# A dilated FIR with gate and projection: from a window planner with two-way splits to a fixed block order with taps i and i+8 in four products

## The chip, the core and the metric

The kernel runs on one core of one Trainium2 chip. Times are device microseconds of that core. One execution is also taken by the hardware profiler; views of its profile and trace are quoted below.

## What is computed

`x` is [2, 16000, 144], `w` is [15, 144, 288], `w_o` is [144, 144], all bf16. A causal convolution with 15 taps, 2 tokens apart, is followed by a gate and a projection:

```python
dil = 2
pad = (K - 1) * dil
xp = jnp.pad(x, ((0, 0), (pad, 0), (0, 0)))
h = sum over i of einsum('btc,cd->btd', xp[:, pad - i*dil : pad - i*dil + T], w[i])
f = h[..., :D]
g = h[..., D:]
z = jnp.tanh(f) * sigmoid(g)
return z @ w_o
```

So h at token t is the sum over i of x[t - 2i] w[i]. The 144 input channels are 128 that fill TensorE's rows ("main") and 16 left over ("rest"); the rests of several taps are stacked into one 128-row operand.

## The kernel before

**Tiling.** Each sequence of 16000 tokens is cut into windows: 15 of 1024 tokens (`k4`), one of 512 (`k2`), one of 128 (`std`). Two k4 windows make a chunk; 16 chunks are run in one loop (L416). A chunk's x is loaded by two transposing DMAs (L136 to L158): `xn` with channels 0 to 127 on the partitions, `xb` with channels 16 to 143, and eight copies within SBUF (L154) stack the last 16 channels, shifted by 0, 4, ... 28 tokens, into `rx`. All of these are issued on SP's queue.

**Fewer products.** A FIR with taps in pairs can be had for two output tokens from three products rather than four: one of a sum of weights, two of differences of x. `unit_k4` (L334) does this twice, so that a window's tokens of one parity, 4 outputs of 128 tokens each, need nine accumulation groups: `a1`, `a2`, `a3`, `c1`, `b1`, `b2`, `b3`, `c2`, `c3`, each of 4 or 5 matmuls of 288 columns in a PSUM bank of its own. The stationary operand is always x or a difference of it, read with a step of 8 tokens (L339); the moving one is a weight or a sum of weights. VectorE makes the differences `en`, `fn`, `gn`, `re` of a whole chunk (L164 to L183) as dense bf16 operations and adds the groups in f32 (L350 to L382); ScalarE copies a1, c1, b1 out of PSUM (L345, L358, L366). `unit_k2` does one such step, `unit_std` none. All matmuls of the convolution are recorded at the helper's line, L319.

**Gate and projection.** ScalarE takes tanh and sigmoid of 4 x 144 outputs (L324, L325), VectorE multiplies (L326). z goes to DRAM (L275) and comes back through two transposing DMAs (L280) as `zta` and `ztb`, 72 channels each; two matmuls of 144 columns a 128-token group (L307, L308) give the output, which ScalarE copies to bf16 (L309) and stores on its own queue. The last chunk transposes z on TensorE instead (L253).

**Order.** The order of the work is left to the framework's scheduler, with two kinds of ordering added by hand: `dma_T` and `dma_plain` (L118, L128) make every transposing DMA wait for the plain ones issued since the last, and plain ones for the last transposing one. The next chunk's differences and the previous chunk's projection are spread over the units of the current chunk (L466 to L473).

Of the kernel before, what the change touches and what calls it, by code (L numbers as in the profile page):

```python
# [8 lines left out]
BF16 = mybir.dt.bfloat16  # L9
# [6 lines left out]
def kernel(  # L16
# [6 lines left out]
):  # L23
    nc = tc.nc
# [4 lines left out]
    assert D2 == 2 * D and w.shape[1] == D  # L29
    CM = 128  # L30
    CR = D - CM
    assert CR == 16 and K == 15
    DH = D // 2
    KV = 8
    KO = 7
    NG = 8
    BOFF = D - P
    HTOK = 32
    assert T % P == 0 and T >= 4 * P
    dep_sync = mybir.DependencyInfo(mybir.DependencyClass.Sync, mybir.DependencyReason.DATA)  # L40
    dep_order = mybir.DependencyInfo(mybir.DependencyClass.NoSync, mybir.DependencyReason.SCHED_ONLY)

    KIND_TOK = {"k4": 8 * P, "k2": 4 * P, "std": P}

    def mk_items():
        items = []
        t = 0
        for kind in ("k4", "k2", "std"):
            n = KIND_TOK[kind]
            while T - t >= n:  # L50
                items.append((kind, t))
                t += n
        assert t == T
        return items

    CTOK = 2 * KIND_TOK["k4"]

    def mk_chunks():
        items = mk_items()
        groups = []  # L60
        i = 0
        while i < len(items):
            j = i
            span = 0
            while j < len(items) and span + KIND_TOK[items[j][0]] <= CTOK:
                span += KIND_TOK[items[j][0]]
                j += 1
            rest = sum(KIND_TOK[it[0]] for it in items[j:])
            if rest < KIND_TOK["k4"]:
                j = len(items)  # L70
            groups.append(items[i:j])
            i = j
        res = []
        for g in groups:
            t_a = g[0][1]
            t_b = g[-1][1] + KIND_TOK[g[-1][0]]
            res.append((g, t_a, t_b))
        return res

    def chunk_geom(t_a, t_b):  # L80
        if t_a == 0:
            R = min((t_b + 15) // 16 * 16, T)
            return R, 0, HTOK
        R = (t_b - t_a + HTOK + 15) // 16 * 16
        return R, t_b - R, 0

    chunk_list = mk_chunks()
    WB = 0
    SLOT = 0
    for (_, t_a, t_b) in chunk_list:  # L90
        R, t_lo, jlo = chunk_geom(t_a, t_b)
        assert t_lo >= 0 and t_lo + R <= T
        WB = max(WB, jlo + R)
        SLOT = max(SLOT, t_b - t_a)
    WB = (WB + 15) // 16 * 16
    SLOT = (SLOT + 15) // 16 * 16
    ZPAD = 16
    all_chunks = [(b, items, t_a, t_b) for b in range(B) for (items, t_a, t_b) in chunk_list]
    NCH = len(all_chunks)
# [3 lines left out]
    xd_pool = ctx.enter_context(tc.tile_pool(name="xd", bufs=2))  # L103
    cp_pool = ctx.enter_context(tc.tile_pool(name="cp", bufs=3))
    y_pool = ctx.enter_context(tc.tile_pool(name="y", bufs=3))
    act_pool = ctx.enter_context(tc.tile_pool(name="act", bufs=2))
    z_pool = ctx.enter_context(tc.tile_pool(name="z", bufs=4))
    zt_pool = ctx.enter_context(tc.tile_pool(name="zt", bufs=2))
    os_pool = ctx.enter_context(tc.tile_pool(name="os", bufs=4))
    ztd_pool = ctx.enter_context(tc.tile_pool(name="ztd", bufs=2))  # L110
    ps_acc = ctx.enter_context(tc.tile_pool(name="ps_acc", bufs=6, space=bass.MemoryType.PSUM))
    ps_out = ctx.enter_context(tc.tile_pool(name="ps_out", bufs=2, space=bass.MemoryType.PSUM))
    dram = ctx.enter_context(tc.tile_pool(name="dram", bufs=1, space=bass.MemoryType.DRAM))

    fence_plain = []
    last_T = [None]

    def dma_T(out_ap, in_ap):  # L118
        ti = nc.sync.dma_start_transpose(out=out_ap, in_=in_ap)  # L119
        for prev in fence_plain:  # L120
            tc.add_manual_dep(ti.ins, prev, dep_sync, reason="dma batching")
        fence_plain.clear()
        if last_T[0] is not None:
            tc.add_manual_dep(ti.ins, last_T[0], dep_order, reason="dma batching")
        last_T[0] = ti.ins.name
        return ti

    def dma_plain(eng, out_ap, in_ap, track=True):  # L128
        di = eng.dma_start(out=out_ap, in_=in_ap)  # L129
        if last_T[0] is not None:  # L130
            tc.add_manual_dep(di.ins, last_T[0], dep_sync, reason="dma batching")
        if track:
            fence_plain.append(di.ins.name)
        return di

    def load_chunk(ci, cp_eng):  # L136
        b, items, t_a, t_b = all_chunks[ci]
        R, t_lo, jlo = chunk_geom(t_a, t_b)
        xn = xa_pool.tile([P, WB], BF16, name="xn")
        xb = xa_pool.tile([P, WB], BF16, name="xb")  # L140
        rx = xa_pool.tile([P, WB], BF16, name="rx")
        wv = jlo + R
        if jlo > 0:
            nc.gpsimd.memset(xn[:, 0:jlo], 0.0)
            nc.gpsimd.memset(xb[:, 0:jlo], 0.0)
# [10 lines left out]
        for l_ in lasts.values():  # L156
            fence_plain.append(l_.ins.name)
# [31 lines left out]
    def derive_chunk(cur):  # L189
        for f in derive_steps(cur):  # L190
            f()
# [325 lines left out]
```

## Time and profile before

| what | value |
|---|---|
| median of 3 runs | 389.66 us (389.6 to 389.79) |
| profiled execution, span from first to last instruction | 387.7 us |
| mean granted TensorE clock | 0.997 |
| ScalarE busy | 189.4 us (49%) |
| DMA | 60.27 MB, 143475 packets, mean 155 GB/s |
| SP's queue (x, rx, z back) | 40.87 MB, 58.7% of 16 engines' time |
| ScalarE's queue (weights, z out, stores) | 18.88 MB, 13.6% |
| convolution matmuls of 288 columns | 2598 |
| projection matmuls and z transposes on TensorE | 526 |

Of a group of instructions the profile gives the number, the mean duration of one, and the idle time of its engine just before them with what ended it. A duration runs from an instruction's start to its end; instructions of one engine can overlap, so that the distance of starts, read from the timeline, is shorter. The chain of waits goes back from the last instruction through whatever released each step: 71% of it is TensorE, 13% VectorE, 5% DMA.

### The profile page before, as it was taken

The numbers are of one execution on the slowest core, as the hardware profiler recorded it, in microseconds if no ns is written. First come the engines' busy times: TensorE is split into PE (matmuls) and PEld (weight loads), VectorE is DVE, ScalarE is ACT, GpSimd is POOL, SyncE is SP. The second block draws the span as 40 slices with busy tenths as digits, with TensorE's granted clock in tenths as the row PEclk, the third lists the DMA queues.
The fourth block names the chain that finished last, engine by engine and source line by source line (L and its number), as shares of the span: only waits on it lengthen the run. The fifth ranks groups of instructions, "written<-read, shape, count | busy, mean of one in ns | idle before, by whom it ended". The sixth has DMA issues, their size and how long they took to land.

```text
span 387.7 us, 8354 instructions
## 1 busy us (share of the span) xinstructions
PE 364.3 (94%) x3124; PEld 354.1 (91%) x3124; DVE 331.1 (85%) x753; ACT 189.4 (49%) x448; POOL 4.7 (1%) x28
## 2 busy tenths in 40 slices
PE   0669999999999999999999999999999999999995
PEld 0468998999999999999989999999999999999984
DVE  3489999998989999899859989999898989897651
ACT  4223445446454644546444454546545454654544
POOL 3000000000000000000000000000000000000000
PEclk9999999999999999999999999999999999999998
DMA  5865794596858859598798979696877969590602
GB/s 154 141 124 104 153 188 87 149 213 170 182 150 156 165 164 191 161 171 175 174 175 132 203 155 198 164 218 137 189 149 174 166 162 200 129 148 30 188 16 110
DMA packets 143475, 60.27 MB, mean 155 GB/s; under 512 B 131275, under 2 KB 133819, under 8 KB 143435
## 3 DMA queue, kind: packets, MB, share of 16 engines
q1 hardware_dynamic: 132764, 40.87, 58.7%
q10 hardware_dynamic: 10671, 18.88, 13.6%
q8 instruction: 24, 0.39, 0.4%
q14 instruction: 16, 0.13, 0.1%
HBM read 1.29 MB, written 18.03 MB: 50 GB/s over the span
## 4 chain that ended last, share of the span: by engine, by line
PE 71%; DVE 13%; DMA 5%; ACT 5%; issue 3%; ACTq 1%; SPq 1%; DVEq 0%
PE out_ps L307 4%; PE out_ps L308 3%; DMA xb<-in_x_dram 3%; ACT th L324 2%; ACTq L129 1%; DMA rx<-xb 1%; ACT sg L325 1%; PE v_ps L319 1%; DMA wo_p<-in_w_dram 1%; DVE en L166 1%; PE yo_ps L319 1%; DVE fn L176 1%; DVE re L171 1%; PE ye_ps L319 1%; SPq L119 1%
## 5 line engine op out<-in xcount | busy, mean ns | idle before, releaser
L319 PEld LDWEIGHTS <-gn 128*128 128x128 bf16 x900 | 116.0, 144 | 0.5 <-issue 0.3
L319 PEld LDWEIGHTS <-en 128*128 128x128 bf16 x540 | 67.0, 141 | 3.5 <-issue 2.6
L319 PEld LDWEIGHTS <-fn 128*128 128x128 bf16 x480 | 61.2, 144 | 2.6 <-DVE fn L176 1.8
L319 PEld LDWEIGHTS <-xn 128*128 128x128 bf16 x302 | 36.1, 136 | 13.6 <-DMA xn<-in_x_dram 11.8
L307 PE MATMUL out_ps<-wo_sb,zta 72*128 72x144 bf16 x237 | 38.7, 226 | 1.5 <-ACT os_2884 L309 0.7
L308 PE MATMUL out_ps<-wo_sb,ztb 72*128 72x144 bf16 x237 | 37.9, 227 | 0.0
L319 PEld LDWEIGHTS <-re 112*128 112x128 bf16 x248 | 35.3, 143 | 1.2 <-DVE re L171 1.1
L308 PEld LDWEIGHTS <-ztb 72*128 72x128 bf16 x237 | 31.4, 143 | 5.2 <-issue 2.3
L307 PEld LDWEIGHTS <-zta 72*128 72x128 bf16 x237 | 32.8, 144 | 0.1
L171 DVE TENSOR_TENSOR re<-rx 128x2078 bf16<-128x2078 bf16 (+1 forms) x16 | 19.3, 1206 | 5.8 <-DMA rx<-xb 5.8
L166 DVE TENSOR_TENSOR en<-xn 128x2078 bf16<-128x2078 bf16 (+1 forms) x16 | 19.3, 1205 | 1.9 <-DMA xn<-in_x_dram 1.9
L319 PEld LDWEIGHTS <-rx 128*128 128x128 bf16 (+1 forms) x128 | 18.0, 142 | 1.9 <-DMA rx<-xb 1.8
L182 DVE TENSOR_TENSOR gn<-en 128x2074 bf16<-128x2074 bf16 (+1 forms) x16 | 19.3, 1206 | 0.1
L176 DVE TENSOR_TENSOR fn<-xn 128x2076 bf16<-128x2076 bf16 (+1 forms) x16 | 19.3, 1204 | 0.0
L319 PE MATMUL a_192<-ss,xn 128*128 128x288 bf16 x4 | 1.2, 447 | 11.8 <-DMA xn<-in_x_dram 11.8
L229 DVE COPY s_main<-w_all 128x288 bf16<-128x288 bf16 x1 | 0.2, 234 | 6.6 <-DMA w_all<-in_w_dram 6.6
L260 DVE COPY zt_sb<-zt_ps 72x512 bf16<-72x512 bf16 (+1 forms) x7 | 2.6, 394 | 3.7 <-PE zt_ps L258 3.7
L146 POOL MEMSET rx<- 128x32 bf16 x16 | 1.8, 122 | 302.3 <-PE a_449 L319 33.3
L319 PE MATMUL v_ps<-s_main,xn 128*128 128x288 bf16 x32 | 4.7, 286 | 0.0
L319 PE MATMUL h_ps<-w_all,xn 128*128 128x288 bf16 x30 | 4.7, 286 | 0.0
L319 PE MATMUL yo_ps<-w_all,en 128*128 128x288 bf16 x32 | 4.6, 286 | 0.0
L319 PE MATMUL ye_ps<-wo_neg,en 128*128 128x288 bf16 x28 | 4.4, 286 | 0.0
(1922 smaller groups left out, 987.8 us busy)
## 6 DMA issues: line engine op xcount, KB each, us to landing
rx<-xb SPq DMA_DIRECT2D x14, 65.0 KB, 2.7
rx<-xb SPq DMA_DIRECT2D x14, 64.8 KB, 2.6
rx<-xb SPq DMA_DIRECT2D x14, 64.5 KB, 4.0
rx<-xb SPq DMA_DIRECT2D x14, 64.2 KB, 2.8
rx<-xb SPq DMA_DIRECT2D x13, 64.9 KB, 2.9
rx<-xb SPq DMA_DIRECT2D x13, 64.6 KB, 2.6
rx<-xb SPq DMA_DIRECT2D x13, 64.4 KB, 3.0
rx<-xb SPq DMA_DIRECT2D x13, 64.1 KB, 3.2
```

Of the source, the lines that this page charges most:

```text
L119: ti = nc.sync.dma_start_transpose(out=out_ap, in_=in_ap)
L129: di = eng.dma_start(out=out_ap, in_=in_ap)
L166: nc.vector.tensor_tensor(out=en[:, 0:wv - 2], in0=xn[:, 2:wv], in1=xn[:, 0:wv - 2], op=ALU.subtract)
L171: nc.vector.tensor_tensor(out=re[:, 0:wv - 2], in0=rx[:, 2:wv], in1=rx[:, 0:wv - 2], op=ALU.subtract)
L176: nc.vector.tensor_tensor(out=fn[:, 0:wv - 4], in0=xn[:, 4:wv], in1=xn[:, 0:wv - 4], op=ALU.subtract)
L182: nc.vector.tensor_tensor(out=gn[:, 0:wv - 6], in0=en[:, 4:wv - 2], in1=en[:, 0:wv - 6], op=ALU.subtract)
L260: nc.vector.tensor_copy(out=sb[:, 0:ne], in_=ps[:, 0:ne])
L307: nc.tensor.matmul(po[:, e, :], lhsT=ck["zta"][0:DH, sl], rhs=wo_sb[:, 0, :], start=True, stop=False)
L308: nc.tensor.matmul(po[:, e, :], lhsT=ck["ztb"][0:DH, sl], rhs=wo_sb[:, 1, :], start=False, stop=True)
L319: nc.tensor.matmul(ps[:, 0:D2], lhsT=l, rhs=r, start=(i == 0), stop=(i == n - 1))
L324: nc.scalar.activation(out=th[:, 0:ne, :], in_=y_ap[:, :, 0:D], func=ACT.Tanh)
L325: nc.scalar.activation(out=sg[:, 0:ne, :], in_=y_ap[:, :, D:D2], func=ACT.Sigmoid)
```

## The change

The two sequences are laid behind each other with a gap of 32 zero tokens and cut into 21 blocks of 1536 tokens: 32 periods of 48 tokens. Every instruction is pinned to the order in which the program gives it (`K_`).

- **Split.** Taps i and i + 8 (16 tokens apart) are taken together: four products V, A for `S` (sum), `D` (difference) and twice `E` give three outputs 16 tokens apart in a period of 48. Inside each product the taps 4 apart (8 tokens) are split again: a V group of 4 matmuls, and two A groups of 4 main matmuls (3 in one case) and one rest matmul, from `S4`, `D4`, `E4` and `Sr`, `Dr`, `Er`. An accumulator `acc` is a pair of PSUM banks; three pairs are in use, and two banks for the projection.
- **Derived operands.** `S`, `D`, `E`, `Sr`, `Dr`, `Er` are made by VectorE from xn and rx through the view `per`, which reads for each pair of tokens u the 32 periods, 48 tokens apart, 2 tokens from each, and written densely. The stationary operand of every matmul is then 128 contiguous columns.
- **Joins.** ScalarE takes eight accumulators of a block out to bf16 (two negated); VectorE joins them in bf16 SBUF operations of 1152 elements and takes the last four accumulators straight from PSUM. W2 and the other combined weights carry a factor 2, undone by `scale=0.5` in the gate.
- **z.** The block's z lies in SBUF as [128, 12 x 144], padded to 1792, and is transposed from there in one DMA on SP's queue; two matmuls with a shifted copy of w_o (`wo_ab`) make each 128-token group. z's buffer in DRAM and the fences between plain and transposing DMAs are gone.
- **Queues.** x, rx, the z transposes and the output stores are all on SP's queue, in program order; the weights and 16 pieces of w_o are loaded on ScalarE's queue ahead of the first block. The stores write runs of 288 bytes.

```diff
-        y_sb = y_pool.tile([P, 4, D2], F32, name="y4")
-        a1 = acc_tile("a1")
-        mm_group(a1, [(st(xn, -8 * j), ss[:, j, :]) for j in range(4)])
...
-        for (dst, c0) in ((zta, 0), (ztb, DH)):
-            srcz = bass.AP(zs_dram.tensor, zs_dram[slot, r0, c0].offset, [[D, ntok], [1, P]])
-            dma_T(dst[:, 0:ntok], srcz)
...
+    def load_x(bi):
+        loads, zeros = segs(bi)
+        cur = dict(bi=bi)
+        for (nm, c0) in (("xn", 0), ("xb", D - P)):
+            t_ = xa_pool.tile([P, XA], BF16, name=nm)
+            cur[nm] = t_
+            for (a, e) in zeros:
+                K_(nc.gpsimd.memset(t_[:, a:e], 0.0))
+            for (col, b, tk, n) in loads:
+                src = bass.AP(x.tensor, x[b, tk, c0].offset, [[D, n], [1, P]])
+                K_(nc.sync.dma_start_transpose(out=t_[:, col:col + n], in_=src))
+        blocks[bi] = cur
+    def load_r(bi):
+        cur = blocks[bi]
+        rx = xr_pool.tile([P, XA], BF16, name="rx")
+        for i in range(8):
+            K_(nc.sync.dma_start(out=rx[CR * i:CR * (i + 1), 16:XW], in_=cur["xb"][P - CR:P, 16 - 2 * i:XW - 2 * i]))
+        cur["rx"] = rx
+    def per(t_, s, wd):
+        return t_[:, s:s + NB_TOK].rearrange("p (k u e) -> p u k e", k=NP, e=2)[:, 0:wd // 2]
+    def uke(t_):
+        return t_[:].rearrange("p (u k e) -> p u k e", k=NP, e=2)
+    def tt(out_, a, b, op):
+        return K_(nc.vector.tensor_tensor(out=out_, in0=a, in1=b, op=op))
...
+        def s4(nm, wd):
+            s = cur[nm]
+            tt(mk(nm + "4", wd)[:], s[:, 8 * NP:(8 + wd) * NP], s[:, 0:wd * NP], ALU.subtract)
+        def sS():
+            tt(uke(mk("S", 30)), per(xn, HALO - 14, 30), per(xn, HALO + 2, 30), ALU.add)
+        def sD():
+            tt(uke(mk("D", 30)), per(xn, HALO - 14, 30), per(xn, HALO + 2, 30), ALU.subtract)
+        def sE():
+            tt(uke(mk("E", 46)), per(xn, HALO + 2, 46), per(xn, HALO - 30, 46), ALU.subtract)
+        def sS4():
+            s4("S", 22)
+        def sD4():
+            s4("D", 22)
+        def sE4():
+            s4("E", 38)
+        def sSr():
+            tt(uke(mk("Sr", 16)), per(rx, HALO, 16), per(rx, HALO + 16, 16), ALU.add)
+        def sDr():
+            tt(uke(mk("Dr", 16)), per(rx, HALO, 16), per(rx, HALO + 16, 16), ALU.subtract)
+        def sEr():
+            tt(uke(mk("Er", 32)), per(rx, HALO + 16, 32), per(rx, HALO - 16, 32), ALU.subtract)
+        return dict(S=sS, D=sD, E=sE, S4=sS4, D4=sD4, E4=sE4, Sr=sSr, Dr=sDr, Er=sEr)
...
+    load_x(0)
+    load_r(0)
+    load_x(1)
+    wo_ab = const.tile([P, 16, D], BF16)
+    K_(nc.gpsimd.memset(wo_ab[:], 0.0))
+    for j in range(8):
+        o = 16 * j
+        K_(nc.scalar.dma_start(out=wo_ab[o:P, j, :], in_=w_o[0:P - o, :]))
+        K_(nc.scalar.dma_start(out=wo_ab[0:CR + o, 8 + j, :], in_=w_o[P - o:D, :]))
+    zs = [const.tile([P, ZW], BF16, name=f"z{i}") for i in range(2)]
+    for z_ in zs:
+        K_(nc.gpsimd.memset(z_[:, NCL * D:ZW], 0.0))
+    load_r(1)
+    load_x(2)
...
+    for nm in ("S", "D", "S4", "D4"):
+        st0[nm]()
+    for (m, op) in ((0, ALU.add), (1, ALU.subtract)):
+        tt(G[m][:, 0:7, :], w_all[:, 0:7, :], w_all[:, 8:15, :], op)
+        K_(nc.scalar.copy(out=G[m][:, 7, :], in_=w_all[:, 7, :]))
+        tt(H[:, m], G[m][:, 0:4, :], G[m][:, 4:8, :], ALU.add)
+        tt(Wr[:, m, 1, :], wrA[:], wrB[:], op)
+        K_(nc.scalar.mul(out=Wr[:, m, 0, :], in_=Wr[:, m, 1, :], mul=-1.0))
+    K_(nc.scalar.mul(out=W2[:, 0:8], in_=w_all[:, 0:8], mul=2.0))
+    K_(nc.scalar.mul(out=W2[:, 8:K], in_=w_all[:, 8:K], mul=2.0))
+    for (m, src) in ((2, wrA), (3, wrB)):
+        K_(nc.scalar.mul(out=Wr[:, m, 1, :], in_=src[:], mul=2.0))
+        K_(nc.scalar.mul(out=Wr[:, m, 0, :], in_=src[:], mul=-2.0))
+    for nm in ("Sr", "Dr", "E", "E4", "Er"):
+        st0[nm]()
+    tt(H[:, 2], W2[:, 0:4, :], W2[:, 4:8, :], ALU.add)
+    tt(H[:, 3, 0:3], W2[:, 8:11, :], W2[:, 12:15, :], ALU.add)
+    K_(nc.vector.tensor_copy(out=H[:, 3, 3, :], in_=W2[:, 11, :]))
...
+    def pe_V(cur, m):
+        acc = ps_acc.tile([P, 2, 512], F32, name="acc")
+        t_ = cur[XN[m]]
+        for b1 in range(2):
+            jobs = []
+            for i in range(4):
+                o = XB[m] + SH[m] + 4 * b1 - 2 * i
+                jobs.append((t_[:, o * NP:(o + 4) * NP], H[:, m, i, :]))
+            mm_bank(acc[:, b1, 0:D2], jobs)
+        return acc
+    def pe_A(cur, m, b2):
+        acc = ps_acc.tile([P, 2, 512], F32, name="acc")
+        t_ = cur[XN[m] + "4"]
+        r_ = cur[XN[m] + "r"]
+        for b1 in range(2):
+            jobs = []
+            for i in range(4):
+                wt = Gw(m, i if b2 else i + 4)
+                if wt is None:
+                    continue
+                o = XB[m] + SH[m] + 4 * b1 - 2 * i - (0 if b2 else 8)
+                jobs.append((t_[:, o * NP:(o + 4) * NP], wt))
+            o = RB[m] + SH[m] + 4 * b1 + 8 * b2
+            jobs.append((r_[:, o * NP:(o + 4) * NP], Wr[:, m, b2, :]))
+            mm_bank(acc[:, b1, 0:D2], jobs)
+        return acc
...
+    def act_ev(dst, acc, sign=1.0):
+        K_(nc.scalar.activation(out=dst, in_=acc[:, :, 0:D2], func=ACT.Copy, scale=sign))
+    def bc(v):
+        return bass.AP(v.tensor, v.offset, [list(v.ap[0]), [0, 2]] + [list(p) for p in v.ap[1:]])
+    def gate_act(cur, f):
+        th = g_pool.tile([P, 4, D], BF16, name="th")
+        sg = g_pool.tile([P, 4, D], BF16, name="sg")
+        y = cur["y"]
+        K_(nc.scalar.activation(out=th[:], in_=y[:, 4 * f:4 * f + 4, 0:D], func=ACT.Tanh, scale=0.5))
+        K_(nc.scalar.activation(out=sg[:], in_=y[:, 4 * f:4 * f + 4, D:D2], func=ACT.Sigmoid, scale=0.5))
+        cur["g", f] = (th, sg)
+    def gate_mul(cur, f):
+        th, sg = cur["g", f]
+        z = zs[cur["bi"] % 2]
+        tt(z[:, 4 * f * D:(4 * f + 4) * D], th[:].rearrange("p a d -> p (a d)"), sg[:].rearrange("p a d -> p (a d)"),
+           ALU.mult)
+    def start_zT(cur):
+        zT = zt_pool.tile([P, ZW // P, P], BF16, name="zT")
+        K_(nc.sync.dma_start_transpose(out=zT[:], in_=zs[cur["bi"] % 2][:]))
+        cur["zT"] = zT
+        cur["os"] = os_pool.tile([P, NCL, D], BF16, name="os")
+    def outproj(cur, g):
+        po = ps_out.tile([P, 512], F32, name="po")
+        for j in range(3):
+            c = 3 * g + j
+            blk, o = divmod(D * c, P)
+            mm_bank(po[:, j * D:(j + 1) * D], [(cur["zT"][:, blk, :], wo_ab[:, o // 16, :]),
+                                               (cur["zT"][:, blk + 1, :], wo_ab[:, 8 + o // 16, :])])
+        K_(nc.scalar.copy(out=cur["os"][:, 3 * g:3 * g + 3, :].rearrange("p a d -> p (a d)"), in_=po[:, 0:3 * D]))
+    def store(cur):
+        for (p0, n, ncl, b, tk) in store_segs(cur["bi"]):
+            for r in range(2):
+                for e in range(2):
+                    dst = bass.AP(out.tensor, out[b, tk + 2 * r + e, 0].offset, [[PER * D, n], [4 * D, ncl], [1, D]])
+                    s = RW * r + 2 * p0 + e
+                    K_(nc.sync.dma_start(out=dst, in_=cur["os"][s:s + 2 * (n - 1) + 1:2, 0:ncl, :]))
...
+        cur["y"] = y_pool.tile([P, NCL, D2], BF16, name="y")
+        y = cur["y"]
+        a = pe_V(cur, 0)
+        if prev:
+            gate_act(prev, 2)
+            Ap = prev["A31"]
+            tt(prev["y"][:, 2:4, :], prev["U0"][:, 1], Ap[:, :, 0:D2], ALU.subtract)
+            Ap = prev["A30"]
+            tt(prev["y"][:, 0:2, :], prev["U0"][:, 0], Ap[:, :, 0:D2], ALU.add)
+        v1 = c_pool.tile([P, 2, D2], BF16, name="v1")
+        act_ev(v1[:], a)
+        dv("S")
+        if prev:
+            gate_mul(prev, 2)
+        a = pe_V(cur, 1)
+        if prev:
+            gate_act(prev, 0)
+        vm = c_pool.tile([P, 2, D2], BF16, name="vm")
+        act_ev(vm[:], a)
+        dv("D")
+        if prev:
+            gate_mul(prev, 0)
+            start_zT(prev)
+        a1 = sb("a1")
+        a = pe_A(cur, 0, 1)
+        act_ev(a1[:, 1], a)
+        dv("E")
+        a = pe_A(cur, 0, 0)
+        act_ev(a1[:, 0], a, -1.0)
+        dv("S4")
+        dv("D4")
+        am = sb("am")
+        a = pe_A(cur, 1, 1)
+        act_ev(am[:, 1], a)
+        m1 = sb("m1")
+        tt(m1[:], a1[:], bc(v1[:]), ALU.add)
+        dv("E4")
+        a = pe_A(cur, 1, 0)
+        act_ev(am[:, 0], a, -1.0)
+        dv("Sr")
+        dv("Dr")
+        dv("Er")
+        if bi + 2 < NBLK:
+            load_r(bi + 2)
+        if bi + 3 < NBLK:
+            load_x(bi + 3)
+        a = pe_V(cur, 2)
+        v0 = c_pool.tile([P, 2, D2], BF16, name="v0")
+        act_ev(v0[:], a)
+        mm_ = sb("mm")
+        tt(mm_[:], am[:], bc(vm[:]), ALU.add)
+        tt(y[:, 4:8, :].rearrange("p (a b) d -> p a b d", a=2), m1[:], mm_[:], ALU.subtract)
+        a = pe_V(cur, 3)
+        vi = c_pool.tile([P, 2, D2], BF16, name="vi")
+        act_ev(vi[:], a)
+        pp = sb("pp")
+        tt(pp[:], m1[:], mm_[:], ALU.add)
+        u2 = sb("u2")
+        tt(u2[:], pp[:], bc(v0[:]), ALU.add)
+        gate_act(cur, 1)
+        u0 = sb("u0")
+        tt(u0[:], pp[:], bc(vi[:]), ALU.subtract)
+        cur["U0"] = u0
+        if prev:
+            outproj(prev, 0)
+        a = pe_A(cur, 2, 1)
+        tt(y[:, 10:12, :], a[:, :, 0:D2], u2[:, 1], ALU.add)
+        gate_mul(cur, 1)
+        if prev:
+            outproj(prev, 1)
+        a = pe_A(cur, 2, 0)
+        tt(y[:, 8:10, :], u2[:, 0], a[:, :, 0:D2], ALU.subtract)
+        if prev:
+            outproj(prev, 2)
+        cur["A31"] = pe_A(cur, 3, 1)
+        if prev:
+            outproj(prev, 3)
+            store(prev)
+        cur["A30"] = pe_A(cur, 3, 0)
+        prev = cur
```

More of the change, by code (lines that the diff above doesn't have):

```diff
@@ L6 @@
 from concourse._compat import with_exitstack
-from concourse.masks import make_identity
 BF16 = mybir.dt.bfloat16
@@ L45, in mk_items @@
[L45 to L78, printed above, removed]
@@ L112 @@
+    ps_acc = ctx.enter_context(tc.tile_pool(name="ps_acc", bufs=3, space=bass.MemoryType.PSUM))
     ps_out = ctx.enter_context(tc.tile_pool(name="ps_out", bufs=2, space=bass.MemoryType.PSUM))
[L113 to L126, printed above, removed]
@@ new lines @@
+    K_(nc.scalar.activation(out=warm[:], in_=warm[:], func=ACT.Sigmoid))
+    load_x(0)
[10 more added lines that the diff above has]
+        K_(nc.gpsimd.memset(z_[:, NCL * D:ZW], 0.0))
```

453 lines of the change are left out of this document (101 added, 352 removed).

## Prediction

> **What bounds the kernel now.** I read the busy table first, then the slices, then one stretch of the timeline from the middle.
>
> ```profile
> span 387.7 us, 8354 instructions
> ...
> PE 364.3 (94%) x3124; PEld 354.1 (91%) x3124; DVE 331.1 (85%) x753; ACT 189.4 (49%) x448; POOL 4.7 (1%) x28
> ...
> PE   0669999999999999999999999999999999999995
> ...
> DVE  3489999998989999899859989999898989897651
> ```
>
> TensorE is full from the fourth slice to the last but one; the granted clock is 0.997. VectorE is close behind. So a change pays only if TensorE gets less to do and no other engine passes it.
>
> ```profile
> 202.29 0.65 PE L319 MATMUL c_3267<-aos,en 128*128 128x288 bf16 x4
> ...
> 202.78 0.65 PE L319 MATMUL b_3278<-aes,en 128*128 128x288 bf16 x4
> ```
>
> Four matmuls of 288 columns start 0.49 us ahead of the next four: 0.123 us each, although one takes 286 ns from start to end. The eight 144-column matmuls from 200.88 take 0.55 us to the next group: 0.069 each. These paces, not the durations, are the price of TensorE.
>
> ```profile
> 239.70 0.44 DVE L350 TENSOR_TENSOR q_3886<-a_3880,a1s 128x288 f32<-128x288 f32 x1
> 240.07 0.45 DVE L354 TENSOR_TENSOR q_3894<-a_3888,a1s 128x288 f32<-128x288 f32 x1
> 240.43 1.23 DVE L176 TENSOR_TENSOR fn<-xn 128x2076 bf16<-128x2076 bf16 x1
> 241.58 0.45 DVE L326 TENSOR_TENSOR z_3629<-th,sg 128x576 bf16<-128x576 bf16 x1
> 241.95 0.45 DVE L360 TENSOR_TENSOR u_3903<-c1s,q_3886 128x288 f32<-128x288 f32 x1
> ```
>
> VectorE operations also start before the one in front has ended: 0.37 us apart for 288 f32 elements, 1.15 for 2076 bf16, 0.37 for 576 bf16. That is 0.073 us plus 1.04 ns an element in f32 and 0.52 in dense bf16. All VectorE costs below use this.
>
> **TensorE after.** A block of 1536 tokens has 4 V groups of 8 matmuls (32) and 8 A groups of 10, one of them short by 2 (78): 110 of 288 columns, plus 24 of 144. 110 x 0.123 + 24 x 0.069 = 15.2 us. There are 32032 / 1536 = 21 blocks, so 319 us, against 2598 x 0.123 + 526 x 0.069 = 356 now. **Gain on TensorE: 37 us.** The stationary operands become contiguous; their loads are hidden now and stay so.
>
> **VectorE after, one block, 22 operations.** Four evictions joined from PSUM at 576 (0.073 + 0.600 = 0.67): 2.69. Six bf16 joins of 1152 (0.67 each): 4.04; the operand repeated over an outer dimension is taken at the dense rate. Three gate products (0.37): 1.12. S4, D4, E4, dense runs of 704, 704 and 1216: 1.59. Sum 9.44. The rest are the six new differences that also reorder: S, D (960 elements each), E (1472), Sr, Dr (512), Er (1024), together 5440 elements and 6 x 0.073 = 0.44 of fixed cost. They write densely but read two bf16, then jump 48 elements (96 bytes), in both inputs.
>
> No row shows VectorE reading so. From below: dense, 0.52 ns an element. An element a cycle, as the f32 rows pay, is 1.04. That jumps cost something shows only on another engine, in the loads of stationary operands with steps of 1, 4 and 8 elements (three windows of the groups by form):
>
> ```profile
> L319 PEld LDWEIGHTS <-xn 128*128 128x128 bf16 x9 | 0.8, 98 | 0.1
> ...
> L319 PEld LDWEIGHTS <-en 128*128 128x128 bf16 x30 | 3.4, 115 | 0.3
> ...
> L319 PEld LDWEIGHTS <-gn 128*128 128x128 bf16 x12 | 1.6, 144 | 0.0
> ```
>
> 98, 115 and 144 ns: the wider the jump, the slower. Upper end: pairing lost and the 144 / 98 of the widest jump on top, 1.04 x 1.47 = 1.53 ns. I take 1.25, about the middle of 1.04 and 1.53, because the jump here is six times the widest that the rows show and every 4-byte word has one. Ends kept for the range: 0.52 and 1.53.
>
> [...]
>
> At 1.25 the six cost 0.44 + 6.80 = 7.24 us, and VectorE needs 9.44 + 7.24 = **16.7 us a block, against TensorE's 15.2.** (Dense: 12.7.) VectorE becomes the bound.
>
> **Stalls on VectorE.** Its order is fixed, so waits add up. Two operations read the result of the one right in front: 0.12 each, the difference of duration and pace with a little for the signal. The last wait of a block is y01 on A30: from y48 the chain runs tanh and sigmoid (1.3 on ScalarE; 0.69 each, overlapping), the first output copy (0.5), the third output group (two PSUM buffers, so it waits for that copy; 0.6 with its drain), A31 (1.23), output group (0.4), A30 with its drain (1.2), some 5.4 us with the signals. VectorE's own work from there is pp, u2, u0, y11, gm1, y9, y23: 4.5, with the stalls 4.75. Stall 0.65. **Period 16.7 + 0.9 = 17.6 us.** Other waits are covered: y23 by TensorE running ahead, the gate products by S and D in front of them. Without that cover (dense S and D) they cost under 1 us a block, when TensorE is the bound anyway.
>
> **ScalarE:** 8 evictions of 576 (0.55 apart), 6 gate halves (0.60), 4 copies of 432 (0.43): 9.7 us. Covered.
>
> **DMA and SP's queue.** Gone are z's trip through DRAM, its two transposes and the fences between plain and transposing DMAs. SP now issues per block one transpose of z, 8 copies for rx, 2 transposes of x, 4 stores, each waiting in line behind the other.
>
> ```profile
> 220.01 8.00 SPq L129 DMA_DIRECT2D rx<-xb  x8
> 229.93 1.92 SPq L119 DMA_TRANSPOSE zta<-zs_dram  x1
> ...
> 240.32 5.93 SPq L129 DMA_DIRECT2D rx<-xb  x8
> ```
>
> Eight rx copies take 5.9 to 8.0 us of issue; a transpose 1.4 to 4.1 in this window; a store on ScalarE's queue 0.34 to 0.56, though in longer runs than the new 288-byte ones. Low: 5.9 + 1.4 + 3 x 1 + 1.4 = 11.7; high: 8.0 + 4.1 + 4.6 + 3.6 = 20.3. I take 15, under the period. A transposed source in SBUF is in no row; I give it the landing of ztb, 4.7 us. VectorE hands z over 5 us into a block, so it lands near 10, where TensorE reaches the first output group (V, V, four A, V, V: 8.9). Just covered; a landing 3 us later is a rival.
>
> **Start.** ScalarE issues 6 weight loads (4 x 0.55 + 1.23 + 0.87 = 4.3), a table load and its first sigmoid (1.5), then 16 pieces of w_o at some 0.6: at 16.2 us it first copies the centre tap that H waits for. VectorE then goes through the weights and block 0's remaining differences (5.4 at 1.25) and is free at 26.7. Block 0 lacks the previous block's four operations: 16.7 - 2.1 + 0.2 = 14.8. Block 1 begins at 41.5.
>
> **Sum.** 41.5 + 19 x 17.6 + 15.3 for the last block, which derives nothing and runs at TensorE's pace: 391.2. Tail: y01 0.75, gate 1.3 and 0.45, transpose 4.7, output groups and copies 2.9, 8 stores (two segments) issued over 4.2 after the first and 2.6 to land: 16.9. Span 408; the median lies 2.0 above the profiled span of 387.7, so **410 us**. Each 0.1 ns an element is 21 x 544 ns = 11.4 us; the break-even is near 1.07 ns.
>
> **Rivals.**
> 1. *The jumps are free* (pairs are fetched at full rate): TensorE is the bound at 15.2 us, block 1 begins at 36.6, 36.6 + 289 + 15.3 + 17 + 2 = **360**, faster. Decided below about 0.8 ns an element. For: the innermost step is 1. Against: the load rows. 0.21.
> 2. *An element a cycle* (1.04): period 16.4, block 1 at 39.7: 39.7 + 312 + 15.3 + 17 + 2 = **386**, on the edge; 0.85 to 1.15 ns covers 366 to 398. 0.14.
> 3. *SP's queue or the z transpose takes over*: an issue of 5 us and a landing at 8 hold back the output groups, the last PSUM pairs and through the stores the next transpose; SP's 17.2 us (5.0 + 6.6 + 3.2 + 2.4) and the wait for the last copy make 18.1 to 18.8 a block: **420 to 436**, whatever the jumps cost. For: it all sits on one queue in fixed order. Against: 4.7 us rows now. 0.12.
> 4. *Upper end of the jumps* (1.4 to 1.53): 425 to **442**. 0.05.
>
> Forecast (1.15 to 1.4 ns): 0.48, its own range 398 to 425. The range 358 to 430 leaves out the far ends of cases 1, 3 and 4, under 0.2. A measurement of this kernel tells 0.2% from nothing. Faster takes case 1, most of case 2: 0.31; same 0.02; slower 0.67.
>
> **What would show it.** S, D at 1.3 to 1.4 us and E near 2.0 (dense: 0.65 and 0.92) on VectorE; VectorE in the high nineties of per cent per block with TensorE near 86%; periods of 17.6 us; the first output group of a block not waiting long for z's transpose. Wrong if S shows 0.65 us and TensorE stays at nine tenths and more, or if TensorE's waits name the z transpose.

## Result and the profile after

The changed kernel takes **420.65 us** (median of 4 runs, 419.41 to 421.24) against 389.63 for the kernel before, measured beside it: a ratio of 1.0797 (95% interval 1.0777 to 1.0818). It is 8% slower. The forecast was 410 us with a range of 358 to 430. The profiled execution's span is 419.5 us; before it was 387.7. Some runs of one experiment (9) were in a slower state with a lower granted clock (0.93 to 0.95, against 0.99); of it only the fastest run and blocks at full clock are used.

From the page of the changed kernel: the busy line, the slices of TensorE and VectorE, and the granted clock (PEclk, in tenths):

```profile
PE 332.6 (79%) x2814; PEld 264.8 (63%) x2814; DVE 359.5 (86%) x471; ACT 227.2 (54%) x390; POOL 3.7 (1%) x15
...
PE   0059779797897977978979796978879797797931
...
DVE  2199998899999999999998996999899999998520
...
PEclk9997989899999999999998998999899999999985
```

TensorE has 32 us less to do (364.3 to 332.6) and yet no longer stands at nine tenths throughout. VectorE has 28 us more, in 471 instructions rather than 753, and stands at nine tenths nearly everywhere. The bound went from the one engine to the other. The clock row has dips; the mean granted clock is 0.954, against 0.997 before.

The groups of the changed kernel by form (line, engine, operation, tiles and shapes, count, then busy us and mean ns of one, then idle time before):

```profile
L129 DVE TENSOR_TENSOR E<-xn 128x1472 bf16<-128x1472 bf16 x21 | 41.6, 1983 | 0.0
...
L129 DVE TENSOR_TENSOR Er<-rx 128x1024 bf16<-128x1024 bf16 x21 | 30.0, 1428 | 0.0
...
L129 DVE TENSOR_TENSOR S<-xn 128x960 bf16<-128x960 bf16 x21 | 28.3, 1346 | 7.6 <-DMA xn<-in_x_dram 7.6
```

These are three of the jumping differences. S takes 1.35 us for 960 elements; D the same; Sr and Dr 0.79 for 512.

VectorE starts the S of one block after the other at 102.31, 119.63, 136.94, 154.27 us and so on: **17.32 us** is the common period. (The S that runs in a block makes the operand of the next one; "S of block 1" below is the one that runs in block 1, here at 47.26.) Of the 18 distances from S of block 1 on, five are longer: 18.78, 18.95, 19.01, 19.01 and 21.33. One table by stretches shows a common block (188.92 to 206.24) and then a long one (206.24 to 225.25), cut where its third output group begins; columns are length, busy time and instructions of each engine, granted clock, DMA share and GB/s:

```profile
188.92:206.24 17.32, 15.31 (x137) 12.18 (x135) 16.79 (x23) 10.41 (x19) 0.00 (x0) 1.00 0.71 123
206.24:219.50 13.26, 11.34 (x99) 8.97 (x97) 13.12 (x18) 7.62 (x14) 0.00 (x0) 1.00 0.61 102
219.50:225.25 5.75, 5.49 (x38) 4.16 (x38) 3.78 (x7) 2.82 (x6) 0.00 (x0) 0.70 0.71 151
```

In the common block VectorE (third busy time) works 16.79 of 17.32 us, 97%, and TensorE (first) 15.31, 88%. In the last part of the long block the granted clock is 0.70 on the mean (0.50 from 221 to 224 us), and VectorE, which had been full, is idle a third of the time. The timeline of that place, TensorE first, then VectorE:

```profile
219.76 0.54 PE L239 MATMUL po<-wo_ab,zT 128*128 128x144 bf16 x6 [2.18 <-ACT os L305]
...
221.65 0.45 PE L239 MATMUL acc<-Wr,Er 128*128 128x288 bf16 x1
```

```profile
224.57 0.76 DVE L129 TENSOR_TENSOR y<-u,acc 128x576 bf16<-128x576 bf16 x1 [1.68 <-PE acc L239]
```

TensorE waits 2.18 us for an output copy (`os`) on ScalarE. Soon after, a matmul of 288 columns takes 0.45 us instead of 0.29, and y01, the last VectorE operation of the block, waits 1.68 us for A30, the last accumulator, instead of 0.40. TensorE waits for that copy in 18 blocks, in 17 of them for 2.1 to 2.5 us; the clock fell behind four of these waits, in the four blocks of 18.8 to 19.0 us (0.91 on the mean of each, against 1.00 in the common ones).

The block of 21.33 us is another matter. SyncE's queue at that place:

```profile
241.46 9.79 SPq L313 DMA_DIRECT2D out_dram<-os  x12
251.36 1.58 SPq L294 DMA_TRANSPOSE zT<-z  x1
```

The block at the border of the two sequences has 12 stores rather than 4. Their issue takes 9.8 us, the transpose of z stands behind them, and TensorE's first output group waits 4.80 us for it. The clock falls behind this wait too (0.92 on the mean of the block).

**Where the time went**, by the prediction's own terms (predicted, then measured): up to block 1 on VectorE 41.5, 45.3; 19 periods 334.4, 19 x 17.32 + 11.8 = 340.9, where 11.8 is the excess of the five long blocks and small rests; the last block 15.3, 15.0; the tail 16.9, 18.3. Sum 408, 419.5.

### The profile page after: what moved, and what is told of

It is laid out like the page before. It is cut to its first block, busy times and chain, and to the rows that moved or that the text cites. A ratio compares the mean times of both kernels' runs of the same rounds, so it can differ in the third digit from the quotient of the medians.

```text
span 419.5 us, 7230 instructions
## 1 busy us (share of the span) xinstructions
PE 332.6 (79%) x2814; PEld 264.8 (63%) x2814; DVE 359.5 (86%) x471; ACT 227.2 (54%) x390; POOL 3.7 (1%) x15
## 4 chain that ended last, share of the span: by engine, by line
PE 33%; DVE 31%; SPq 13%; DMA 9%; ACT 6%; issue 4%; ACTq 2%; DVEq 0%
PE acc L239 27%; SPq L118 10%; DVE E L129 7%; PE po L239 6%; DMA rx<-xb 5%; DVE D L129 4%; DVE y L129 4%; DVE Er L129 4%; DVE S L129 3%; ACT sg L283 3%; DMA xb<-in_x_dram 2%; SPq L313 2%; DMA zT<-z 2%; ACT os L305 2%; DVE Dr L129 2%
## 5 line engine op out<-in xcount | busy, mean ns | idle before, releaser
L239 PEld LDWEIGHTS <-E 128*128 128x128 bf16 x966 | 93.7, 100 | 23.9 <-issue 2.3
L239 PE MATMUL acc<-W,E 128*128 128x288 bf16 x630 | 106.6, 296 | 2.1 <-DVE y L129 2.1
L239 PE MATMUL po<-wo_ab,zT 128*128 128x144 bf16 x504 | 48.0, 236 | 50.9 <-ACT os L305 38.3
L239 PEld LDWEIGHTS <-S 128*128 128x128 bf16 x504 | 50.2, 100 | 38.8 <-issue 16.2
L129 DVE TENSOR_TENSOR y<-u,acc 128x576 bf16<-128x576 bf16 x63 | 46.0, 751 | 16.3 <-PE acc L239 16.3
L239 PEld LDWEIGHTS <-D 128*128 128x128 bf16 x504 | 50.4, 100 | 14.1 <-issue 0.4
L239 PE MATMUL acc<-G,S 128*128 128x288 bf16 x336 | 53.4, 290 | 3.0 <-ACT v L273 3.0
L239 PE MATMUL acc<-Gm,D 128*128 128x288 bf16 x336 | 54.0, 292 | 0.0
L239 PE MATMUL acc<-Wr,Er 128*128 128x288 bf16 x168 | 49.7, 296 | 0.0
L239 PE MATMUL acc<-H,E 128*128 128x288 bf16 x336 | 44.6, 286 | 0.0
L129 DVE TENSOR_TENSOR E<-xn 128x1472 bf16<-128x1472 bf16 x21 | 41.6, 1983 | 0.0
L129 DVE TENSOR_TENSOR S<-xn 128x960 bf16<-128x960 bf16 x21 | 28.3, 1346 | 7.6 <-DMA xn<-in_x_dram 7.6
L129 DVE TENSOR_TENSOR Er<-rx 128x1024 bf16<-128x1024 bf16 x21 | 30.0, 1428 | 0.0
```

The costliest lines, as they stand in the source:

```text
L129: return K_(nc.vector.tensor_tensor(out=out_, in0=a, in1=b, op=op))
L239: K_(nc.tensor.matmul(ps, lhsT=l, rhs=r, start=(k == 0), stop=(k == n - 1)))
```

## Experiments

All kernels differ from the changed one only by what is shown or told; dots in the code stand for lines not shown. Times are medians; the kernel before, measured beside each, took 389.2 to 390.1. A ratio is to the kernel before, with its 95% interval. "Period" is the common distance between the S operations on VectorE.

**1. Differences without jumps.** The operands are read in one run from the same start, so other tokens are added: this leaves the reordering out, and nothing else.

```diff
-        return t_[:, s:s + NB_TOK].rearrange("p (k u e) -> p u k e", k=NP, e=2)[:, 0:wd // 2]
+        return t_[:, s:s + wd * NP].rearrange("p (u k e) -> p u k e", k=NP, e=2)
```

> Leaves out the reordering: S, D, E, Sr, Dr, Er read as many elements, but side by side, so the operands hold the wrong tokens. Theory (VectorE is the bound, and the jumps make it so): S 0.65 us, E 0.92, VectorE 4.0 us a block less, 13.3 in all; TensorE's 15.2 us becomes the bound, periods of 15.2 to 15.6, and the time falls by 20 x 1.8 = 36 and more to 370 to 385. Rival A (the block is held by the waits between TensorE and ScalarE over the output groups): the period stays over 16.8, the time over 405. Rival B (SP's queue with z's transpose is the bound): S gets short, but the period does not, time 400 to 420.

Measured: 370.62 us, ratio 0.9513 (0.9489 to 0.9537), period 14.97. From its page and its groups:

```profile
PE 323.7 (88%) x2814; PEld 261.6 (71%) x2814; DVE 282.2 (76%) x471; ACT 225.6 (61%) x390; POOL 3.7 (1%) x15
```

```profile
L129 DVE TENSOR_TENSOR E<-xn 128x1472 bf16<-128x1472 bf16 x21 | 19.3, 919 | 0.0
```

E falls from 1983 to 919 ns, S and D to 652, and TensorE is the bound at 15.0 us a block, busy in all of a common one. So the jumps alone decide between 5% faster and 8% slower: 77 us of VectorE's work, 50 us of time.

**2. The second gating behind the output copies.** ScalarE's order is the program's; tanh and sigmoid of the second third stood ahead of the first two output copies, and TensorE's third output group waited for the first of these (2.18 us in the block shown above).

```diff
-        gate_act(cur, 1)
         u0 = sb("u0")
...
+        if prev:
+            outproj(prev, 1)
+        gate_act(cur, 1)
         gate_mul(cur, 1)
-        if prev:
-            outproj(prev, 1)
```

> The two output copies of the previous block go ahead of the middle gate on ScalarE; VectorE's and TensorE's orders stay. Theory: the common period of 17.32 us is VectorE's work and stays within 0.4; the four blocks of 18.8 to 19.0 us come from TensorE's clock falling to half after the 2.2 us wait for the output copy and go away: 7 to 14 us less, 407 to 414. Rival A (waits over the output groups are the bound): period down to 15 to 16, time below 395. Rival C (TensorE has 2.1 us a block to idle wherever that is, and the clock falls just as often): 417 to 421. Rival D (the long blocks come from the DMA): no change.

Measured: 404.25 us, ratio 1.0382 (1.0358 to 1.0406), period 16.85. The waits for the output copy are gone from the middle of the span, the four blocks of 18.8 to 19.0 us are gone with them, and the wait of y01 too. It adds up: 19 x 0.47 = 8.9 us from the period, 6.5 from the four blocks, together 15.4 of the 16.4 won. Slightly more than expected, because the wait of y01 fell as well. The block with 12 stores stayed (20.41).

**3. w_o on GpSimd's queue.** The 16 pieces leave ScalarE's queue, where the first copies of weights stood behind them.

```diff
-        K_(nc.scalar.dma_start(out=wo_ab[o:P, j, :], in_=w_o[0:P - o, :]))
-        K_(nc.scalar.dma_start(out=wo_ab[0:CR + o, 8 + j, :], in_=w_o[P - o:D, :]))
+        K_(nc.gpsimd.dma_start(out=wo_ab[o:P, j, :], in_=w_o[0:P - o, :]))
+        K_(nc.gpsimd.dma_start(out=wo_ab[0:CR + o, 8 + j, :], in_=w_o[P - o:D, :]))
```

> The 16 pieces of w_o are loaded on GpSimd's queue rather than on ScalarE's. Theory (the start waits for ScalarE's issues): the centre tap is copied near 9 us rather than 20.8, the next wait is for rx of block 0, near 20.5; block 1 begins 3 to 5 us earlier, time 415 to 418. Rival: the start is held by the x loads and rx alone, no change beyond 1 us.

Measured: 414.76 us, ratio 1.0653 (1.0628 to 1.0677). In the changed kernel the copy of the centre tap looked so:

```profile
20.78 0.43 ACT L209 COPY G<-w_all 128x288 bf16<-128x288 bf16 x1 [14.10 <-DMA wo_ab<-in_w_o_dram]
```

It now runs at 6.85, 14 us earlier, but S of block 1 only 4.5 us earlier (42.76 for 47.26): the next thing late is the tile `rx` of block 0 (the stacked rests, "the four rows" in some of the texts below), for which Sr waits till 19.27. The rest of the 5.9 us is not the start: TensorE waits for the output copy as before, 16 times for 2.1 to 2.2 us, but in the middle only one block of 18.99 us follows such a wait, where the changed kernel had four.

**4. How far and how often a jump.** Each of the six differences gets another pattern of the same number of elements (other tokens again; this leaves the right reordering out): S in runs of 8 bytes that start off an 8-byte border, D in runs of 8 bytes that start on one, E in runs of 16 bytes, Sr with one input jumping and one dense, Dr in pairs 8 bytes apart, Er in pairs 68 bytes apart.

```diff
+        def hop(t_, off, us, un, ks, kn, en):
+            v = t_[:, off:off + 1]
+            return bass.AP(v.tensor, v.offset, [list(v.ap[0]), [us, un], [ks, kn], [1, en]])
...
-            tt(uke(mk("Er", 32)), per(rx, HALO + 16, 32), per(rx, HALO - 16, 32), ALU.subtract)
+            tt(uke(mk("Er", 32)), hop(rx, 48, 2, 16, 34, 32, 2), hop(rx, 16, 2, 16, 34, 32, 2), ALU.subtract)
```

> One look at durations; the operands hold the wrong tokens. S reads runs of 8 bytes that start 36 bytes into the tile, D the same at 32 bytes, E runs of 16 bytes, all 96 bytes apart; Sr jumps in one input only; Dr jumps by 8 bytes, Er by 68. [...] Theory 2 (a fixed price for each jump, 1.5 ns over the dense rate): S and D 1.0, E 1.2, Er 1.43, Dr 0.79, Sr 0.6 to 0.79. Theory 3 (pairing is lost whenever runs are short): S, D 1.15 and E 1.6. Time by 1: 375 to 395; by 2: 385 to 405.

Measured in one run: 370.72 us, below both of the ranges expected. The groups of this kernel:

```profile
L129 DVE TENSOR_TENSOR Er<-rx 128x1024 bf16<-128x1024 bf16 x21 | 21.9, 1042 | 0.0
L129 DVE TENSOR_TENSOR E<-xn 128x1472 bf16<-128x1472 bf16 x21 | 19.3, 919 | 0.0
L129 DVE TENSOR_TENSOR S<-xn 128x960 bf16<-128x960 bf16 x21 | 18.4, 878 | 6.6 <-DMA xn<-in_x_dram 6.6
L129 DVE TENSOR_TENSOR Sr<-rx 128x512 bf16<-128x512 bf16 x21 | 16.4, 781 | 0.0
```

E in runs of 16 bytes costs what dense costs (919). S in misplaced runs of 8 bytes costs 878 against 652 dense; D in placed ones 741; Dr in near pairs 416, dense. Sr with one jumping input (781) is as dear as with both (792). Er at 68 bytes costs 1042, between dense (685) and the 1428 at 96 bytes. So it is neither the number of inputs nor the reordering as such that is paid for, but the distance between single 4-byte pairs: nothing at 8 bytes, and more at 96 than at 68. (At 68 bytes every second pair also changes its place against an 8-byte border; the two are not separated here.) Theories 2 and 3 don't fit: D in placed runs, at 0.74 us, is below the 1.0 of the one and the 1.15 of the other, E at 0.92 below their 1.2 and 1.6, and Er at 68 bytes, at 1.04, below theory 2's 1.43.

**5. GpSimd does the jumping.** It copies each block's tiles into the order of the products, as 4-byte words, and VectorE reads dense.

```diff
+        K_(nc.gpsimd.tensor_copy(out=u_[:].bitcast(I32).rearrange("p (u k) -> p u k", k=NP), in_=src))
...
-            tt(uke(mk("S", 30)), per(xn, HALO - 14, 30), per(xn, HALO + 2, 30), ALU.add)
+            tt(mk("S", 30)[:], cur["xnu"][:, 8 * RW:23 * RW], cur["xnu"][:, 16 * RW:31 * RW], ALU.add)
```

> Nothing is left out: GpSimd, idle until now, copies xn and rx once per block into the order of the operands (as 4-byte words, 1248 and 1024 of them), and S, D, E, Sr, Dr, Er read them densely. Theory (the jumps on VectorE are the cost): S 0.65, E 0.92, Er 0.68 us, period 14.9 to 15.3 us as with the dense reads, time 368 to 378. Rival A (two engines reading SBUF at once hold each other up): VectorE's operations grow by a tenth or more beside GpSimd's copies, period over 15.5, time 380 to 400. Rival B (GpSimd's copies jump as badly and take over 7 us each): GpSimd becomes the bound, over 400.

Measured: 416.58 us, ratio 1.0679 (1.0657 to 1.0702). The timeline of this kernel says why:

```profile
209.89 2.71 POOL L128 COPY rxu<-rx 128x1024 int32<-128x1024 int32 x1 [10.75 <-DMA rx<-xb]
209.92 0.74 DVE L139 TENSOR_TENSOR y<-u,acc 128x576 bf16<-128x576 bf16 x1
...
213.04 3.27 POOL L128 COPY xnu<-xn 128x1248 int32<-128x1248 int32 x1 [0.43 <-DMA xn<-in_x_dram]
213.16 3.67 DVE L139 TENSOR_TENSOR S<-xnu 128x960 bf16<-128x960 bf16 x1
```

S, which starts beside the copy, ends only with it: 3.67 us for 0.65 of work. D, free of it, takes 0.65 at 217.12. The eviction y, which has one input in PSUM, keeps its 0.74 us beside the other copy. So beside GpSimd's copies S, with both inputs in SBUF, was held, and y, with one in PSUM, was not. By the means, S (1516 ns for 652), the gate products z (1064 for 452) and the joins y and pp (873 for 758, 897 for 751) grew by some 62 us in all, and S waited another 10.6 for the copies to end; the jumps had cost 77. Little is left of the gain. The theory's 368 to 378 us was missed; rival A was right in kind, but had put the hold at a tenth or more and the time at 380 to 400. Copies placed beside evictions alone were not tried.

**6 and 7. The repairs together**, with GpSimd's copies and without them (edits of 2 and 3, with and without that of 5).

> The unfolding on GpSimd, the two output copies ahead of the middle gate, and w_o's pieces on GpSimd's queue behind the first block's unfolding, together. Theory: the period is TensorE's 15.0 us already without the new order, so that change adds little now (0 to 3 us); the earlier start gives 4 to 6. Time 362 to 370, below the kernel before and the dense-read one. Rival: the copies on GpSimd lie in front of w_o and the start is not shorter, 368 to 376.

> The new ScalarE order and w_o on GpSimd's queue, with the jumping reads kept. Theory (VectorE stays the bound; the two gains lie in different places and add): 404.25 - 5.9 = 398.4, 397 to 400, still slower than the kernel before. Rival (both gains are the same slack): 402 to 405.

Measured: 416.15 us with the copies (ratio 1.0663, 1.0641 to 1.0685), a miss, again with S held (mean 1895 ns); **399.66** without them (ratio 1.0241, 1.0214 to 1.0268). The two repairs add up, and the change is still slower than the kernel before: the 16.84 us that VectorE needs per block are left.

**8 to 10. ScalarE does the jumping.** On top of the two repairs, ScalarE copies the x tile for S, D and E once a block, at the block's end (8); rx, "the four-row tile", too (9); the kernel of 8 with the stores behind the next transpose of z (10).

```diff
+        K_(nc.scalar.copy(out=u_[:].rearrange("p (u k e) -> p u k e", k=NP, e=2), in_=src))
...
+        if bi + 2 < NBLK:
+            unfold(bi + 2, "xn", HALO - 30, 39)
         prev = cur
```

> Theory: the six reordering differences are the bound, and an engine that does not hold VectorE can take the hop from them. On top of the two repairs that are already together (second gating behind the first two output projections, the pieces of w_o on GpSimd's queue; 399.7 us), ScalarE copies each block's part of the x tile that S, D and E read into the order of the products (2496 elements, once a block, two blocks ahead, behind the last output copy), and S, D and E read that copy without jumps. From rows: ScalarE's 2304-element copy took 2.11 us, so about 2.3 us a block, which makes ScalarE about 13.5 us of a block; S, D and E fall from 1.34, 1.34 and 1.98 to 0.65, 0.65 and 0.92 us, so VectorE falls from 16.8 to about 14.4 and TensorE with its 15.0 becomes the bound: 19 blocks times 1.85 less than 399.7, so 360 to 370 us, below the kernel before. Rival 1: ScalarE's copy holds VectorE as GpSimd's did; then S or its neighbours show 2 to 3 us and the time stays at 395 to 415. Rival 2: ScalarE pays for the jumps itself (above 4 us a copy), evictions come late, TensorE waits on banks: 375 to 400.

> The same with the four-row tile copied by ScalarE too (2048 elements, in the block before its use, behind the eviction of vm), so that all six differences read without jumps: VectorE about 12.9 us a block, ScalarE about 15.4 by the row of 2304 elements in 2.11 us, above TensorE's 15.0. Theory: the bound moves to ScalarE, and nothing more is won: 368 to 385 us, slower than with the x tile alone. Rival: ScalarE has room between its waits and the time is that of the x tile alone or below, 355 to 367. Second rival: ScalarE's copies hold VectorE: 390 to 415.

> The kernel with the x tile copied by ScalarE, and one edit more: the stores of a block are issued behind the next block's transpose of z on SyncE's queue, rather than ahead of it, so that the block with 12 stores no longer holds that transpose back. Theory: the long block of 20 to 22 us at about 250 us becomes an ordinary one, 3 to 5 us less than the same kernel without the edit: 356 to 366 us. Rival: SyncE's queue is as full as before and the loads of the four rows behind the stores come late instead: same time within 2 us.

Measured: 8 took 411.84 us (ratio 1.0579, 1.0555 to 1.0604), 10 took 410.84 (1.0543, 1.0504 to 1.0583): my theory missed both by more than 40 us. 9 took 441.51 us in its fastest run, above its theory and both its rivals, with a period of 18.86 us at full clock. The timelines of 8 at a block's end, ScalarE and then VectorE:

```profile
217.30 3.29 ACT L128 COPY xnu<-xn 128x2496 bf16<-128x2496 bf16 x1
```

```profile
220.62 0.66 DVE L139 TENSOR_TENSOR S<-xnu 128x960 bf16<-128x960 bf16 x1 [2.00 <-ACT xnu L128]
```

The copy costs 3.29 us, between the 2.3 of dense rows and the more than 4 of rival 2. VectorE's own operations are dense (D 0.65, E 0.92), so rival 1's sign is missing, though its range holds the time. But I had put the copy right ahead of the S that reads it and of the gating that the transpose of z hangs on: VectorE waits 2.0 us in the block shown and 1.5 on the mean, and TensorE waits later for evictions of v (16 us in the middle of the span). Rival 2 is thus right about the late evictions, at a time above its 375 to 400. The common period is 16.92, no gain over 16.84, and not the "some 18 us" of an expectation below. The 12 us above the 399.66 of the repairs alone are the start (S of block 1 at 47.28 for 42.10) and five blocks of 17.5 to 18.3 us; in four of these TensorE waits some 1 us for the transpose of z. In 9 the second copy adds 2.73 us to ScalarE, which is then the busiest engine (15.81 of 18.86 us) and the one VectorE waits for, 4.1 us a block. In 10 the transpose of z went ahead of the 12 stores (issued at 240.77) and a long block remained, one later (21.49): the loads behind the stores were late instead, and the next transpose with them. The rival of 10 was right.

**11 and 12. The copy in parts, where ScalarE waits.** Also on top of the two repairs. Three parts of 832 elements for the block after next, behind the last eviction of am, that of vi and the second output copy (11); two parts for S and D alone, E still jumping (12).

```diff
         act_ev(am[:, 0], a, -1.0)
+        unfold(bi + 2, 0)
...
         act_ev(vi[:], a)
+        unfold(bi + 2, 1)
...
+        if prev:
+            outproj(prev, 1)
+        unfold(bi + 2, 2)
+        gate_act(cur, 1)
```

> The run with the x tile copied by ScalarE showed the copy at 3.29 us (1.28 ns an element) and VectorE's own operations at their dense times, D 0.65 and E 0.92, but the copy stood at the end of the block, right ahead of the S that reads it, in the one place where VectorE and TensorE waited for it: 2.0 us a block, and a period of some 18 us. Here the same copy is cut in three parts of 832 elements (about 1.2 us each by those rows) and put where ScalarE waits for TensorE: behind the last eviction of am, behind the eviction of vi and behind the second output copy, for the block after next. Theory: nothing waits for it any more, and the three engines stand at 14.4 (VectorE), 14.9 (ScalarE, 11.3 plus 3.6) and 15.0 us (TensorE) a block; with some friction a period of 15 to 16, so 399.7 less 19 times 0.85 to 1.85: 365 to 384 us, below the kernel before. Rival: ScalarE is full, evictions and gatings come late one after the other, period 16.9 or more: 398 to 410.

> As the kernel with the copy in three parts, but only the part of the x tile that S and D read is copied (1472 elements, two parts of about 1.0 us, behind the last eviction of am and behind that of vi); E keeps its jumps. VectorE 16.8 less 1.4 is 15.4 us a block, ScalarE 11.3 plus 2.0 is 13.3, TensorE 15.0. Theory: VectorE bounds at 15.4 to 16.0, so 372 to 385 us, between the kernel with three parts and the one without a copy, if ScalarE has room there; rival: ScalarE is the bound of the kernel with three parts, and this one is the faster of the two by 5 us or more; second rival: its copies hold others up all the same, 395 to 410.

Measured: 11 takes **382.01 us**, ratio 0.9787 (0.9758 to 0.9817): faster than both kernels, by some 2% than the one before. 12 takes 388.27 (ratio 0.9963, 0.9941 to 0.9984), as good as the kernel before. From the page of 11, busy line and chain of what ended last, and its groups:

```profile
PE 327.0 (86%) x2814; PEld 261.9 (69%) x2814; DVE 311.1 (82%) x471; ACT 288.3 (76%) x453; POOL 12.2 (3%) x31
...
PE 47%; ACT 29%; DMA 9%; DVE 5%; issue 5%; SPq 3%; ACTq 0%; DVEq 0%
```

```profile
L132 ACT COPY xnu<-xn 128x832 bf16<-128x832 bf16 x63 | 77.0, 1230 | 11.0 <-DMA xn<-in_x_dram 11.0
```

VectorE is 5% of the chain, TensorE 47%, ScalarE 29%. The period is 15.34, 0.37 above the 14.97 at which TensorE ran alone in experiment 1; 0.20 of it is a wait of TensorE for the last y of the block (at 108.57). Beside the copies VectorE keeps its times (y from m and mm 0.76 us at 103.44, beside a copy from 103.02 to 104.24), so ScalarE did not hold it there. The total is at the upper end of what was expected because the start got longer: S of block 1 is at 48.40 us against 42.10 without copies, since ScalarE's copies of block 1's x tile wait 10.1 us for it, with the copies of weights behind them; and the block with 12 stores takes 22.2. In 12 the period is 15.77, within 15.4 to 16.0; its time missed the expected 372 to 385 by 3 us for the same two reasons.

## Why the prediction held, step by step

- **The price of a jump (right, shown; its exactness in part luck).** Taken at 1.25 ns an element. The ground was "about the middle" of two bounds, the upper one an estimate carried over from TensorE's loads; it would have served 1.2 or 1.35 as well, and no row or run then gave the price. Two dense rows of experiment 1 (652 ns at 960, 919 at 1472) give 0.52 ns an element and 150 ns fixed; with these, S is (1346 - 150) / 960 = 1.25 and Er (1428 - 150) / 1024 = 1.25, or 2.50 ns for a pair of bf16 96 bytes from the next. Experiment 1 takes exactly this away and the sign of the result turns. In experiment 4 a pair at 68 bytes cost (1042 - 150) / 512 = 1.74, and with one input jumping by 96 bytes a pair of Sr cost (781 - 150) / 256 = 2.46, as much as with both in the changed kernel, (792 - 150) / 256 = 2.51.
- **VectorE as the bound (right).** 16.7 us a block predicted; 17.32 less the 0.40 of y01 and two times 0.12 is 16.7. TensorE's 15.2 came out at 14.97 where it bounds alone (experiment 1).
- **The stall of y01 (right in kind, a little too large).** 0.65 predicted, 0.40 measured; the period 17.32 instead of 17.6, which is -5.3 us over 19 blocks.
- **Long blocks (missed, +11.8 us).** The sum took 19 equal periods. I had followed the wait of the third output group for the first output copy, but only as a link in the chain of y01, and had not asked what the clock does behind such a wait: 0.91 on the mean of each of the four blocks of 18.8 to 19.0 us. Experiment 2 takes the wait away, and these four go. Why four and not all is not shown: equal waits had different ends. In the changed kernel the clock fell behind four of 17; in experiment 3, where like waits come 4 to 8 us earlier, behind two of 16 (matmuls of 288 columns at 0.44 us for 0.29). It is not the bare length of the wait, since waits of 2.18 and 2.20 us stand on both sides.
- **The block with 12 stores (missed, 4 of the 11.8).** The prediction counted SyncE's queue as 4 stores a block and 8 at the end, and overlooked the border of the sequences. In a common block that queue issues for some 13.5 us (15 taken). Rival 3 was right in this one block only. Experiment 10 shows that the order of the queue alone doesn't mend it.
- **The start (too short by 3.8).** ScalarE was to reach the centre tap at 16.2; it did at 20.78, held in the pieces of w_o. Experiment 3 shows that this was worth 4.5 us before another wait took over.
- **The tail (too short by 1.4).** The transpose landed in 4 us (4.7 taken), but the output groups and copies took 3.7 (2.9 taken) and the 8 stores issued at 0.75 us each (0.6 taken).
- **Rivals.** 1, 2 and 4 fall with the measured 1.25. Rival 1's price was 360; experiment 1, its case, gave 370.62: TensorE the bound as written, with the long start (block 1 at 40.4 rather than 36.6) and the 12 stores (22.5 us) that the sum lacked too.

The size of the error, 10.65 us, is thus not in the disputed step but in the ends and in the blocks that aren't like the others. It is also a difference of errors: start, long blocks and tail were 17.0 us too short, the 19 periods 5.3 too long. The range of 358 to 430 holds faster and slower kernels alike, so that it held says little; the forecast's own 398 to 425 and its signs (S 1.35, E 1.98, VectorE 97% and TensorE 88% of a common block) say more.

## What to carry to other kernels

When work is moved from a full engine to one with 15% room, price the new access pattern on that engine first: 0.1 ns an element was 11 us of VectorE's work here (21 x 5440 elements), and a reordering in single 4-byte pairs 96 bytes apart made each difference about twice as dear. If the order must change, let an engine with idle places do it, in parts that fit into its waits; what one copy lost at the end of a block, three parts in the right places won. And look for the block that is not like the others (the border of the batch, the first, the last) before multiplying a period.

## What was not expected of the hardware

- The distance counted: single pairs 8 bytes apart cost what dense ones cost (416 and 419 ns for 512 elements), 68 bytes apart 1.74 ns each, 96 bytes apart 2.50; runs of 16 bytes cost nothing over dense (experiment 4).
- One input that jumps by 96 bytes cost VectorE as much as two (781 ns in experiment 4, 792 in the changed kernel, for 512 elements).
- Beside a GpSimd copy of 1248 words a VectorE operation with two SBUF inputs ended only with it (3.67 us for 0.65), while one with an input in PSUM kept its 0.74 us beside a copy of 1024 words (experiment 5); beside a ScalarE copy one with two SBUF inputs kept its 0.76 us (experiment 11).
- ScalarE paid for the jumps too, but less over its dense price: from 832 to 2496 elements its copy grows by (3289 - 1230) / 1664 = 1.24 ns an element, against (2106 - 1867) / 288 = 0.83 in its two dense copies of weights (2304 and 2016 elements).
- Four of 17 waits of TensorE of 2.1 to 2.5 us were followed by a lower clock (two of 16 in experiment 3); in the block shown it was 0.70 on the mean up to the block's end, 5.7 us later.
